# Attention and a gated MLP on one core: every dense product, the scores and P V moved into 64x64 tiles of TensorE, with a new order of the work

## The chip, the cores and the metric

The kernel runs on one core of one Trainium2 chip. The metric is the device time of one launch in microseconds (us). Before the change the median of three runs is 158.33 us (157.89 to 158.91).

## The reference, cut to what matters

S is 2048 tokens of D = 448, in bf16. There are H = 16 heads of 28 columns, each token attends to itself and to seven earlier tokens at distances 2, 4, ..., 14, and F is 1792.

```python
xn = layernorm(x)                               # (x - mean) / sqrt(var + 1e-5)
qkv = xn @ wqkv                                 # q, k, v of 16 heads
logits = q . k[pos - 2 * (0..7)] / sqrt(28)     # -1e9 where that position is negative
o = softmax(logits) @ v ;  s = o @ wo
g = silu(gelu(xn @ w1 + b1) @ w2 + b2)
return x + s * g
```

## The kernel before, in words

**Layout.** Even and odd tokens are kept in two halves of 1024 positions, so that the dilation of 2 becomes a window of eight neighbours. There are 16 token tiles of 128 rows and four chunks of 512 tokens (four tiles each).

**Dense work.** D = 448 is three and a half times 128. Products with that contraction (the projections `qk_rows` L526 and `vproj` L550, and the first layer `ff1` L585) therefore run as seven half steps of 64 rows. `pair` (L477) runs two jobs at once, one in the upper and one in the lower 64 rows of the array, each writing all 128 columns to its own PSUM bank. After four steps the two jobs swap halves, and so banks: since two row tiles must not write one bank at the same time, the second part waits for the first one's last products. The signal goes through a no-op on another engine's queue (`told`, L489 to L493): TensorE tells the no-op's engine, which tells TensorE back. `HOPS` (L20) says whose queue: GpSimd alone for chunks 0 and 1, SyncE or GpSimd later. `first_batch` (L504) starts tiles 0 and 1 in the full array, as their weights land. The second layer (`ff2_part` L616) and the output product (`final_part` L792) have contractions of 14 and 4 times 128 and run in the full array, one product a step.

**Attention.** The tokens are cut into nine blocks of four windows of 57 (one of 56) queries; a window sees 64 keys. For a block, `scores_of` (L666) makes 64 products of 57 columns with 32 rows and 64 columns of the array each (one head's 28 rows padded to 32), into four banks. ScalarE takes their exponential (L687), VectorE or GpSimd multiplies by the mask (L693, `MASK_ON` L21), and `values_of` (L697) makes 64 products for P V in tiles of 64 rows by 32 columns. The value tile holds a column of ones beside each head, so that the sum of the weights comes out with the product; `output_of` (L713) brings that sum to the right partitions with two 32x32 transposes and a reciprocal on VectorE and multiplies (L719 to L733). Values are copied by DMA from token tiles to window tiles (`dma_sb` L352, issued on GpSimd's queue, line L354 in the profile). `VISITS` (L24) groups scores and P V into visits, to change the tile shape seldom.

**What sets the order.** Every step is a task with a cost, dependencies, buffers and a priority, given to `_Plan` (L45). A greedy list scheduler (`run`, L89) picks the order on each engine once, and `emit` (L146) writes the instructions in that order. Each engine then runs its queue in order: an instruction that waits holds all behind it. The priorities stand in `PRIO` and `LATER` (L270 to L294). The chip's own times play no part after that.

**Queues that the change touches.** SyncE issues the loads, the DMA transposes of `xn` and of q and k (`dma_T`, L358) and the stores. GpSimd's queue holds in the beginning: the identity, the bias load (L347), memsets (L319), the mask patterns (L839 to L846), the value copies (L354), the reciprocal roots of tiles 4 to 15 (L425, L426), and the no-ops (L490).

Of the kernel before, what the change touches and what calls it, by code (L numbers as in the profile page):

```python
# [8 lines left out]
F32 = mybir.dt.float32  # L9
BF16 = mybir.dt.bfloat16  # L10
ALU = mybir.AluOpType
# [6 lines left out]
TILED = 30  # L18
SAME = 20
HOPS = ("POOL", ("SP", "POOL"))  # L20
MASK_ON = (("DVE", "POOL"), (0.4, 1.2))  # L21


def VISITS(bs):  # L24
    out = [[("S", b)] for b in bs[:2]]
    for i, b in enumerate(bs):
        out.append([("P", b)] + [("S", c) for c in bs[i + 2:i + 3]])
    return out
# [11 lines left out]
class _Task:  # L40
    __slots__ = ("eng", "cost", "deps", "fn", "prio", "take", "give", "slots",
                 "start", "end", "on", "ndep", "users", "tail", "seq", "table", "limit", "mode", "out")


class _Plan:  # L45
# [7 lines left out]
    def add(self, eng, cost, fn, deps=(), prio=0, take=(), give=(), tail=0.0, table=(), limit=None,  # L53
            mode=128):
# [5 lines left out]
        t.mode, t.out = mode, None  # L60
# [27 lines left out]

    def run(self):  # L89
# [6 lines left out]
        self.mode = 128  # L96
        ready = [t for t in self.tasks if not t.ndep]
        order = []
        while ready:
# [14 lines left out]
            tiled = first[2] == "PE" and self.mode < 64  # L114
            at, t, e, c = min(near, key=lambda k: (-k[1].prio - (TILED if tiled and k[1].mode < 64 else SAME if k[2] == "PE" and k[1].mode == self.mode else 0),
# [4 lines left out]
            if e == "PE" and t.fn is not None:  # L120
                self.mode = t.out or t.mode
# [43 lines left out]
def kernel(  # L165
# [67 lines left out]
    v_tok = [sb(f"v_tok{t}", [P, H, 32]) for t in range(9)]  # L233
    v_tok = v_tok[8:] + v_tok[1:8] + v_tok[:8]
    oT = sb("oT", [P, KT, S])
# [4 lines left out]
    m_gen, m_first, m_mid = [sb(n, [P, 2, 4, NW]) for n in ("m_gen", "m_first", "m_mid")]  # L240
    m1 = [sb(f"m1_{i}", [P, 2, NW]) for i in range(3)]
# [4 lines left out]
    def ring(name, n, shape, dt=BF16, fifo=False):  # L246
# [4 lines left out]
    p_E = ring("E", 8, [P, 512], fifo=True)  # L251
    p_dt = ring("dt", 2, [P, 512], F32)
# [10 lines left out]
    p_v = ring("v", 6, [P, H, 32], fifo=True)  # L263
# [7 lines left out]
        "project": (49.5, 205, 104, 52.5,),  # L271
        "project2": (147, 150, 101, 61,),
        "values": (89.5, 62.5, 21, 58,),
        "attn": (185, 179.5, 78, 174.5, 106.5, 106, 138.5, 136.5, 32.5,),
        "ff1": (185, 180, 84.5, 176.5, 66.5, 64.5, 156.5, 189.5, 203, 146, 76, 114.5, 77.5, 179.5,
            75.5, 118.5, 180.5, 14.5, 163, 68, 151, 115.5, 194.5, 167.5, 180, 188.5, 86, 93,),
        "gelu": (62.5, 22.5, 95, 92.5,),
        "ff2": (144, 162.5, 103.5, 142.5, 44.5, 112.5, 67, 5, 89, 106.5, 101.5, 75, 74, 55, 11.5,
            6.5,),
        "final": (140, 19.5, 70.5, 47, 112, 34.5, 23.5, 142.5, 73, 53, 198.5, 188.5, 81.5, 126.5,  # L280
            180, 71,),
        "norm": (37.5, 132, 179.5, 129.5, 74.5, 99, 161, 69, 63, 62, 43.5, 73, -5.5, 90, 133.5,
            150,),
        "loads": (166.5, 166, 188, 139.5, 54.5,),
        "stats": (47.5, -60, 180.5, 23, 127, 56, 188.5, 77, 197.5, -13.5, 185, 205.5, 138, 14, 52.5,
            138.5,),
        "turn_x": (108.5, -1, 28, 116, 210, 116.5, 131.5, 160, 41.5, 79.5, 70, 119, -4.5, 74.5,
            132.5, 111,),
        "turn_qk": (68.5, 112, 174.5, 90, 80, 6, 149.5, 60.5, 4, 140.5, 199.5, 96.5, 103, 166.5,
            140, 156,),  # L290
        "move_v": (81.5, 95, 23, 95, 18.5, 26.5, 8, 128, 29.5,),
        "copies": (50, 119.5, 58.5, 76, 32.5, 135.5, 43, 1, 87, 79.5, 129, 77, 32, 41.5, 135,),
    }
    LATER = {"swap": 135, "qk": 165, "v": 29.5, "gelu": 30.5, "exp": 55.5, "mask": -60, "pv": 45, "recip": -16.5, "os": 54.5, "y": 153.5, "tanh": 182.5, "g": 58, "sg": 183, "o": 120.5}  # L294
# [45 lines left out]
    t_vw = [plan.add("DVE", 0.08, memset("vector", v[:, :, DH:], 1.0), [t_on], prio=96) for v in v_tok[:9]]  # L340
# [4 lines left out]
    def dma(eng, dst, src, kb, prio, deps=(), issue=0.5, rate=350.0):  # L345
        def fn(_):
            {"SP": nc.sync, "ACT": nc.scalar, "POOL": nc.gpsimd}[eng].dma_start(dst, src)  # L347
        a = plan.add(eng, issue, fn, [t_on] + list(deps), prio)
        return plan.add("DMA", kb / rate, lambda _: None, [a], prio, tail=1.7)
# [16 lines left out]
    def load_x(t0, n, prio, eng="SP", deps=()):  # L366
        d = dma(eng, x_sb[:, t0:t0 + n, :],
                rows(x_half, t0 * P, n * P).rearrange("(t p) d -> p t d", p=P), 112 * n, prio, deps,
                rate=270.0 if t0 < TPC else 350.0)
# [11 lines left out]
    def load_w(kt, prio):  # L381
        t_w.append([dma("SP", w_in[:, kt, :], A_wqkv[kt * P:(kt + 1) * P, :], 336, prio, rate=270.0)])
# [6 lines left out]
    t_w.append([dma("SP", w_in3[:64], tails[:, 0:3:2, :], 112, PRIO["loads"][3], rate=270.0),  # L389
                dma("SP", w_in3[64:], tails[:, 1:3, :], 112, PRIO["loads"][3], rate=270.0)])  # L390

    t_b1z = plan.add("POOL", 0.1, memset("gpsimd", b1r[:], 0.0), [t_on], prio=99)
    t_b1r = dma("POOL", b1r[:NMT], B_b1.rearrange("(m f) -> m f", f=P), 4, 94.5, [t_b1z])
    t_b1r.tail = 5.0
# [41 lines left out]
    def norm(t, prio):  # L436
# [12 lines left out]
        for i in range(2):  # L449
            def f3(k, i=i):  # L450
                xn, tp = buf(p_xn, a), half_bank(buf(p_b, (halves or [k])[0]))
                for kt in (2 * i, 2 * i + 1):
                    nc.tensor.transpose(tp[:, kt, :], xn[:, kt * P:(kt + 1) * P], ident[:])
            halves.append(plan.add("PE", 0.13 if t else 0.22, f3, [twice if i else a, t_ident] + halves, prio, take=() if i else (p_b,),
                                   give=((p_xn, a, 0),) if i else (), tail=0.15))
# [13 lines left out]

    def together(top, bottom):  # L470
        return [(f(), g()) for f, g in zip(top, bottom, strict=True)]
# [5 lines left out]
    def pair(a, b, prio, early=False):  # L477
# [5 lines left out]
        def f1(k):  # L483
# [3 lines left out]
                     tail=0.15, mode=64)  # L487

        def f2(k):  # L489
            held["told"] = (nc.gpsimd if k.on == "POOL" else nc.sync).nop()  # L490
            for i in held["last"]:
                behind(held["told"], i)
# [474 lines left out]
```

## Time and profile before

| what | value |
|---|---|
| median of three runs | 158.33 us (157.89 to 158.91) |
| the profiled execution's own time | 157.98 us |
| its span (first to last instruction) | 156.2 us |
| TensorE busy | 150.1 us, 2204 products |
| VectorE busy | 113.2 us |
| ScalarE busy | 83.3 us |
| GpSimd busy | 74.7 us |
| first layer's first product (L591) | starts at 13.24 us |
| first scores visit (L677) | starts at 45.55 us |
| last TensorE product | ends at 151.7 us |

"Busy" counts time in which the engine works on an instruction. PE is TensorE, PEld its weight loads, DVE VectorE, ACT ScalarE, POOL GpSimd, SP SyncE. A line such as L627 is the line of the kernel that made the instruction; for helpers (L319 memset, L347 and L354 DMA) it is the helper's line. A product's duration in the rows (some 350 ns) is its latency. Products overlap, so the pace is read from start to start.

### The profile page before, as it was taken

Reading aid. Unit: us, or ns where it says so; the run is one execution under the profiler, and the core shown is the slowest. Engines: PE = TensorE matmul, PEld = TensorE weight load, DVE = VectorE, ACT = ScalarE, POOL = GpSimd, SP = SyncE. Lnnn points to the kernel's source line nnn. Section 1 sums busy time; section 2 is a strip of 40 time slices with the busy share of each in tenths; the row PEclk is TensorE's granted clock in tenths of the full one; section 3 lists DMA queues with packets and bytes.
Section 4 is the critical chain, followed back from the end, with each engine's and each line's share of the span. In section 5 each row is a group of like instructions: output and inputs, shape, how many; then the busy total and the mean of one; then the engine's idle time right before and its main releaser. Section 6 shows DMA issues by size and latency. Waiting matters only on the chain.

```text
span 156.2 us, 5305 instructions
## 1 busy us (share of the span) xinstructions
PE 150.1 (96%) x2204; PEld 77.8 (50%) x2204; DVE 113.2 (72%) x259; ACT 83.3 (53%) x149; POOL 74.7 (48%) x123
## 2 busy tenths in 40 slices
PE   6999999999999999999999999999999999999980
PEld 2544454444455555455554644455556444545570
DVE  4789551486266758997799895109899996998992
ACT  3245867378889416444634149782496587051220
POOL 7854856000459408839261098389599780000000
PEclk9999999999999999999999999999999999999999
DMA  4999969999749443099039822123300100200211
GB/s 156 329 317 315 167 124 187 237 269 307 141 95 166 64 82 90 10 192 138 4 83 85 131 70 73 38 76 83 105 0 4 34 31 29 63 4 0 68 36 43
DMA packets 33575, 17.36 MB, mean 111 GB/s; under 512 B 25331, under 2 KB 32387, under 8 KB 33552
## 3 DMA queue, kind: packets, MB, share of 16 engines
q1 hardware_dynamic: 31472, 14.03, 41.3%
q0 software_dynamic: 1936, 2.88, 8.5%
q8 instruction: 17, 0.28, 0.8%
q10 hardware_dynamic: 144, 0.11, 0.2%
q14 instruction: 6, 0.05, 0.1%
HBM read 7.06 MB, written 1.84 MB: 57 GB/s over the span
## 4 chain that ended last, share of the span: by engine, by line
PE 80%; DVE 8%; DMA 3%; POOL 2%; issue 2%; ACT 1%; SPq 1%; DVEq 0%; ACTq 0%; POOLq 0%
PE bank L627 23%; PE bank L591 22%; PE bank L532 11%; PE bank L796 7%; PE bank L556 6%; PE bank L677 4%; PE bank L709 4%; PE bank L327 3%; DMA xnT<-xn 3%; POOL v L354 2%; DVE sg L801 2%; DVE o L807 1%; DVE w_in L659 1%; ACT E L687 1%; DVE xn L438 1%
## 5 line engine op out<-in xcount | busy, mean ns | idle before, releaser
L627 PE MATMUL bank<-w,h 128*128 128x448 bf16 (+1 forms) x238 | 45.2, 342 | 0.0
L591 PE MATMUL bank<-xnT,w 64*128 64x512 bf16 x392 | 44.7, 376 | 0.0
L595 ACT ACTIVATE h<-bank,b 128x512 bf16<-128x512 f32 x56 | 34.0, 689 | 12.9 <-PE bank L591 12.8
L354 POOL DMA_DIRECT2D v<-v_tok x52 | 27.6, 538 | 19.8 <-PE bank L709 9.0
L693 POOL TENSOR_TENSOR E<-E,m_gen 128x456 bf16<-128x456 bf16 x24 | 26.7, 1139 | 11.7 <-ACT E L687 9.5
L627 PEld LDWEIGHTS <-h 128*128 128x128 bf16 x238 | 22.3, 98 | 18.1 <-issue 0.4
L591 PEld LDWEIGHTS <-w 64*128 64x128 bf16 x392 | 19.1, 94 | 22.7 <-issue 1.1
L532 PE MATMUL bank<-w_in,xnT 64*128 64x448 bf16 (+1 forms) x212 | 24.3, 350 | 0.1
L687 ACT ACTIVATE E<-bank 128x456 bf16<-128x456 f32 (+1 forms) x36 | 17.0, 555 | 9.1 <-PE bank L677 9.1
L655 ACT ACTIVATE t<-y 128x448 f32<-128x448 f32 x15 | 8.7, 578 | 17.4 <-DVE y L649 17.4
L719 DVE STREAM_TRANSPOSE dt<-bank 128x480 f32<-128x480 f32 (+1 forms) x18 | 12.1, 671 | 5.6 <-PE bank L709 5.6
L532 PEld LDWEIGHTS <-xnT 64*128 64x128 bf16 (+1 forms) x212 | 10.6, 94 | 10.9 <-issue 1.1
L314 DVE CAST qk_tok<-bank 128x448 bf16<-128x448 f32 x16 | 9.4, 613 | 6.8 <-PE bank L532 6.8
L796 PE MATMUL bank<-wo,oT 128*128 128x448 bf16 (+1 forms) x68 | 14.1, 342 | 0.0
L312 ACT CAST qk_tok<-bank 128x448 bf16<-128x448 f32 x16 | 8.3, 533 | 10.6 <-PE bank L532 10.0
L556 PE MATMUL bank<-w_in,xnT 64*128 64x448 bf16 (+1 forms) x106 | 13.4, 349 | 0.0
L649 DVE TENSOR_TENSOR y<-bank,b 128x448 f32<-128x448 f32 x15 | 9.3, 620 | 4.9 <-PE bank L627 4.9
L728 DVE STREAM_TRANSPOSE dt<-rd 128x480 f32<-128x480 f32 (+1 forms) x18 | 12.1, 673 | 0.5
L733 DVE TENSOR_TENSOR oT<-bank,dt 128x456 bf16<-128x456 f32 (+1 forms) x18 | 11.3, 630 | 0.5
L404 DVE BATCH_NORM_STATS2 st<-x_sb 128x6 f32<-128x448 bf16 x16 | 9.6, 603 | 2.4 <-DMA x_sb<-in_A_x_dram 2.4
L438 DVE TENSOR_SCALAR xn<-x_sb,mv,rstd 128x448 bf16<-128x448 bf16 x16 | 6.3, 394 | 6.0 <-POOL rstd L426 5.8
L796 PEld LDWEIGHTS <-oT 128*128 128x128 bf16 x68 | 6.3, 98 | 6.3 <-issue 0.8
(62 smaller groups left out, 128.9 us busy)
## 6 DMA issues: line engine op xcount, KB each, us to landing
out_dram<-o SPq DMA_DIRECT2D x15, 112.0 KB, 1.7
w<-in_B_w_dram SPq DMA_DIRECT2D x2, 784.0 KB, 7.2
w<-in_B_w_dram SPq DMA_DIRECT2D x2, 672.0 KB, 7.0
x_sb<-in_A_x_dram SPq DMA_DIRECT2D x3, 448.0 KB, 6.3
v<-v_tok POOLq DMA_DIRECT2D x20, 64.0 KB, 2.5
w_in<-in_A_wqkv_dram SPq DMA_DIRECT2D x3, 336.0 KB, 4.3
w<-in_B_w_dram SPq DMA_DIRECT2D x4, 112.0 KB, 6.5
wo<-in_A_wo_dram POOLq DMA_DIRECT2D x4, 98.0 KB, 4.2
```

Of the source, the lines that this page charges most:

```text
L354: nc.gpsimd.dma_start(dst(k), src())
L532: return nc.tensor.matmul(ps[:, :D], xnT[r, kt, cs], w, start=start, stop=stop)
L556: return nc.tensor.matmul(ps[:, :D], xnT[r, kt, k0:k0 + P], w, start=start, stop=stop)
L591: return nc.tensor.matmul(ps[:], w1[r, kt, ms], xnT[r, kt, cs], start=start, stop=stop)
L595: nc.scalar.activation(buf(p_h, own, i)[:], buf(p_b, own, i)[:], ACT.Gelu_apprx_tanh, bias=b1[:, mt:mt + 1])
L627: nc.tensor.matmul(ps[:, :n], buf(*h_at[(c, mt)])[:, j * P:(j + 1) * P], w2[:, mt, cs], start=(mt == 0 and not biased), stop=(mt == NMT - 1))
L687: nc.scalar.activation(buf(p_E, k)[:, :n], buf(p_b, a, at + hl)[:, :n], ACT.Exp, scale=SCALE)
L693: (nc.gpsimd if k.on == "POOL" else nc.vector).tensor_tensor(out=E[:, :n], in0=E[:, :n], in1=m[:, :n], op=ALU.mult)
L719: nc.vector.transpose(buf(p_dt, k)[:, :32 * m], buf(p_b, po, i)[:, :32 * m])
L728: nc.vector.transpose(buf(p_dt, d)[:, :32 * m].rearrange("p (b c) -> p b c", c=32), buf(p_rd, r)[:, :m].unsqueeze(2).to_broadcast((P, m, 32)))
L733: nc.vector.tensor_tensor(out=oT[:, :, q0:q0 + 2 * nq], in0=buf(p_b, po, i)[:, :n].rearrange("p (l q) -> p l q", l=4), in1=buf(p_dt, d)[:, ...
L796: nc.tensor.matmul(ps[:, :n], oT[:, kt, t * P:(t + 1) * P], wo[:, kt, cs], start=(kt == 0), stop=(kt == KT - 1))
```

## The change

- **Dense work.** Each job's product is split into two column strips of 64 (`strips`), and `together` issues the four products of two jobs' strips one after the other: four tiles of 64x64 at a time. The second layer and the output product are made in the same way for two token tiles at once, with the swap of halves and its no-op in between (`rows_in_pairs`, `ff2_pair`, `final_pair`). Tiles 14 and 15 keep the full array there.
- **Scores.** A DMA (`queries_of`, four copies of 32 partitions a block, on SyncE) puts the queries of a block into two planes in which every other head is zero. A scores product then has 64 rows (two heads' keys) and 114 columns (the two planes): 32 products a block instead of 64. The three plane buffers are set to zero at the start on GpSimd.
- **Values.** A value tile has 96 columns for two heads, with 32 zeros between them, so that a P V product of 64 columns adds one head and zeros. The zeros and the ones are set by 18 memsets, 14 of them on GpSimd and four on VectorE, where nine on VectorE were. The window tiles grow from 512 to 768 columns.
- **Masks.** All 36 mask products are on VectorE; 28 were on GpSimd. The mask patterns are 57 columns wide (114 before).
- **Order.** The planner loses the grouping of visits, and gets a term for TensorE's instruction fetch. All priorities are new. Scores and P V are tasks of their own; scores of a block stand two blocks ahead of its P V. The attention output goes into the space of `xnT` and of q in `qkT`, since `oT` is gone. Some of the last output sums go to GpSimd.

The core of the diff:

```diff
-TILED = 30
+BLOCK, FETCH = 128, ((0.0, 4.6), (40.0, 3.8))
-MASK_ON = (("DVE", "POOL"), (0.4, 1.2))
+MASK_ON = ("DVE", 0.4)
...
-    v_tok = [sb(f"v_tok{t}", [P, H, 32]) for t in range(9)]
+    v_tok = [sb(f"v_tok{t}", [P, H // 2, 96]) for t in range(9)]
-    oT = sb("oT", [P, KT, S])
+    p_q = ring("q", 3, [P, 2, G, 4 * NW], fifo=True)
...
-    t_vw = [plan.add("DVE", 0.08, memset("vector", v[:, :, DH:], 1.0), [t_on], prio=96) for v in v_tok[:9]]
+    for n, v in enumerate(v_tok[:9]):
+        e, c = ("DVE", 0.13) if n in (1, 8) else ("POOL", 0.25)
+        for ap, x in ((heads(v[:])[:, :, :, DH:], 1.0), (v[:, :, 32:64], 0.0)):
+            t_vw.append(plan.add(e, c, memset("vector" if e == "DVE" else "gpsimd", ap, x), [t_on], prio=96 if n in (1, 2, 3, 8) else 50))
+    t_q0 = [plan.add("POOL", 1.0, memset("gpsimd", q[:], 0.0), [t_on], prio=20) for q in p_q.bufs]
...
+    def strips(out, lhsT, rhs, half, start, stop):
+        n = P if half > 1 else 64
+        return [lambda c=c: nc.tensor.matmul(out[c:c + n], lhsT[:, c:c + n], rhs, start=start, stop=stop) for c in range(0, P, n)]
     def together(top, bottom):
-        return [(f(), g()) for f, g in zip(top, bottom, strict=True)]
+        done = []
+        for f, g in zip(top, bottom, strict=True):
+            done.append([q() for pair in zip(f(), g(), strict=True) for q in pair])
+        return done
...
+    def queries_of(b):
+        q, nq, _ = VIS[b]
+        def fn(k):
+            to = buf(p_q, k)[:].rearrange("(a b r) z g s -> b a r z g s", a=2, b=2)
+            of = qkT[:, 0, :, q:q + 4 * nq].rearrange("(a b r) g s -> b a r g s", a=2, b=2)
+            for z in range(2):
+                for a in range(2):
+                    nc.sync.dma_start(to[z, a, :, z, :, :4 * nq], of[z, a])
+        a = plan.add("SP", 1.5, fn, [t_qk[t] for t in range(q // P, (q + 4 * nq - 1) // P + 1)] + t_q0, PRIO["move_q"][b], take=(p_q,))
...
     def scores_of(b):
+        def fn(banks, i):
+            for g in range(G):
+                for r in range(2):
+                    for w in range(2):
+                        rs = slice(64 * r, 64 * r + 64)
+                        q0, k0 = wins[w][i]
+                        c0 = 2 * g * nq
+                        nc.tensor.matmul(banks[2 * r + i][NK * w:NK * w + NK, c0:c0 + 2 * nq].rearrange("p (z q) -> p z q", z=2),
+                                         qkT[rs, 1, g, k0:k0 + NK], buf(p_q, at)[rs, :, g, q0 - q:q0 - q + nq], start=True, stop=True)
...
     def values_of(b, exps):
+                        for w in range(2):
+                            rs = slice(NK * w, NK * w + NK)
+                            c0, c1 = (2 * g + i) * nq, (2 * g + z) * nq
+                            nc.tensor.matmul(banks[w][64 * r:64 * r + 64, c0:c0 + nq], v[rs, 2 * g + r, 32 * z:32 * z + 64],
+                                             E[rs, c1:c1 + nq], start=(i, g, z) == (0, 0, 0), stop=(i, g, z) == (1, G - 1, 1))
```

In the changed program's queues TensorE has 3364 products and 6728 instructions with their weight loads (2204 and 4408 before). Of the products 784 are first layer, 618 projections, 826 second layer, 236 output product, 288 scores and 576 P V. SyncE gets 36 more DMAs. On GpSimd the bias load is followed by the memsets of two value tiles, those of `row0` and `wo`, the three mask patterns, the memsets of the other five value tiles and of the three query planes, then the first value copy and the first no-op.

## The prediction, as put on record before the changed kernel ran

> **What bounds the kernel now.** I read the page first (busy shares, slices, chain), then TensorE's timeline, then the queues of the engines that feed it.
>
> ```profile
> span 156.2 us, 5305 instructions
> ...
> PE 150.1 (96%) x2204; PEld 77.8 (50%) x2204; DVE 113.2 (72%) x259; ACT 83.3 (53%) x149; POOL 74.7 (48%) x123
> ...
> PE   6999999999999999999999999999999999999980
> ...
> DVE  4789551486266758997799895109899996998992
> ...
> POOL 7854856000459408839261098389599780000000
> PEclk9999999999999999999999999999999999999999
> ...
> q8 instruction: 17, 0.28, 0.8%
> ...
> PE 80%; DVE 8%; DMA 3%; POOL 2%; issue 2%; ACT 1%; SPq 1%; DVEq 0%; ACTq 0%; POOLq 0%
> ```
>
> TensorE is full from 6 to 151 us and is 80% of the chain that ended last. VectorE is at nine tenths in much of the second half. GpSimd (POOL) is busy in the first 10 us, idle soon after.
>
> TensorE's timeline (start, length) shows what its time is made of:
>
> ```profile
> 49.57 8.12 PE L627 MATMUL bank<-w,h 128*128 128x448 bf16 x42
> 57.62 0.68 PE L709 MATMUL bank<-E,v 64*32 64x57 bf16 x64
> 58.23 0.76 PE L677 MATMUL bank<-qkT 32*64 32x57 bf16 x64
> 58.92 2.82 PE L627 MATMUL bank<-w,h 128*128 128x448 bf16 x14
> ```
>
> From start to start, 42 full-array products take 8.05 us: 0.189 us each and about 0.1 us at the change of tile shape. Row pairs of 512 columns (L591) go at 0.216 us a pair (120 from 29.21 to 42.16). That is 0.42 ns a column, so dense work has no slack. The attention visits are different: 64 products of 57 columns in eight tiles stream for 8 x 0.026 = 0.21 us, yet one takes 0.61 to 0.65. Summed over the timeline (scores to the next dense start), the 18 visits take 12.1 us. 0.4 of it is one wait at 114 us; eleven entries add 0.1 each: 12.7 us of work.
>
> **The change part by part.** The sum is against the profiled execution, 157.98 us, 0.35 under the median of 158.33.
>
> *Dense tiles, 0.* 598 groups of four 64x64 products replace the row pairs and most 128x128 products. A row pair costs what one product costs (0.189 at 448 columns), so I take the same for a four. The ends are 0 and, if the columns of a four did not run beside each other, many us: 1 ns a four is 0.6 us. The eight-tile visits stand against that: their first 32 products run at full streaming rate. A four needs four loads of 64 columns per 189 ns; in a scores visit (L677) 64 such loads go through in 0.63 us, 10 ns apart. The Trainium skill says otherwise on two pages: "TensorEngine Tiling (Array Packing)", Restrictions, says that column tiles lose the fast weight load, and "TensorE: Matmul & The Clock Gate", LDWEIGHTS, gives columns/1.2 ns, 53 for 64. One behind the other, four would take 213 ns, and by that estimate 402 fours of 448 columns lose 9.6 us (166.6 us in all); the row of the visits disagrees.
>
> *Visits, -4.8.* Scores become 32 products of 114 columns in four tiles: 8 rounds of 0.050 = 0.40 us. P V is 64 products in four tiles: 16 x 0.026 = 0.42 us if streaming binds, 0.53 if issue does (0.63 less a shape change). I take 0.48, the middle. 9 x 0.88 = 7.9 for 12.7. Ends 4.3 and 5.3.
>
> *Shape changes between dense runs, -1.05.* The timeline has 15 outside the visits, the new order 4: 11 x 0.095. Ends 0 and -1.05.
>
> *The hop on GpSimd, +3.8.* A pair of jobs swaps banks between its two halves, and a no-op on GpSimd or SyncE (L490) carries the signal; for chunks 0 and 1 it must be GpSimd. What GpSimd does before the first one now:
>
> ```profile
> 1.82 0.70 POOL L347 DMA_DIRECT2D b1r<-in_B_b_dram  x1 [0.30 <-POOL b1r L319]
> 2.52 0.48 POOL L319 MEMSET row<- 128x128 bf16 x2
> 2.95 1.58 POOL L319 MEMSET wo<- 128x1792 bf16 x1
> ...
> 6.14 0.19 POOL L839 MEMSET m<- 128x114 bf16 x1
> ...
> 10.21 0.24 POOL L846 TENSOR_SCALAR_AFFINE_SELECT m<-m 64x56 bf16<-64x56 bf16 x1
> 13.21 1.10 POOL L354 DMA_DIRECT2D v<-v_tok  x2 [2.76 <-PE bank L532]
> ```
>
> ```profile
> L490 POOLq EVENT_SEMAPHORE  x37: 17/17/17, 12.2 to 135.7; - x37
> ```
>
> It is done at 10.45 us and waits for TensorE; the first no-op is at 12.2. In the changed program 14 memsets of value tiles, three of query planes (1824 elements) and one value copy stand ahead of the first no-op. Row by row: 2.5 us to the bias DMA; two value tiles 1.0 (64 elements 0.15 and 256 elements 0.31 by the line through 128: 0.20 and 1792: 1.58, gaps included); rows 0.45; wo 1.55; three masks of 57 columns 1.36 each (6.14 to 7.50), now 4.1; five value tiles 2.5; three planes at 1.6, 4.85; copy 0.53. That is 17.5 to 17.7 us. TensorE has issued the first half of its first w1 pair by 12.9 and of a projection pair by 13.8, and the next instruction in its queue waits for that no-op. So it stands from 13.8 to about 17.6: 3.8 us. Ends: 3.0 (value memsets without gaps) and 5 (short strided runs slower). GpSimd's reciprocal roots for tiles 4 to 7 wait in the same queue behind nine copies and come at 23 and 24 us instead of 18.5 and 19.6. Their transposes then land at 26 to 33 us, about when TensorE, being 3.8 late, asks for them: not added again. If TensorE were not late, this would hold it by about as much. The clock is a risk here: the first nine 512-column products have a mean of 631 ns (L327), 376 later (L591), so it starts slow. The skill's page "TensorE: Matmul & The Clock Gate", Part 1, says that an idle window of some 3.4 us brings half clock back; by that, 3.4 us at half speed add 1.7 us (an estimate), and no run here shows such a gap inside the span.
>
> *Instruction refill, +0.5.* TensorE's program grows from 4408 to 6728 instructions, 17 refills of 16 KB to 26. In the trace refills start as close as 3.65, 3.99 and 4.02 us with no gap in TensorE's work; counted by the 256 instructions between them, the shortest stretch is 4.77. In the new order the densest stretches (a P V visit and dense work) take 3.44, 3.6 and 3.7 us at the rates above. A limit of 3.65 costs 0.3 in sum, 4.0 costs 2.2, 4.75 costs 10.4, and no limit 0. I take 0.5, near the shortest seen.
>
> *Masks on VectorE, +0.6.* GpSimd's 28 mask products go to VectorE: 28 x 0.39 = +10.9 us. Off it come stretched products, as the next two rows show (the same operation beside a GpSimd mask and alone; five such and an output sum, 3.5 us), five output sums (2.0), two casts (1.2), seven memsets (0.8): +3.4 net.
>
> ```profile
> 124.72 1.46 DVE L659 SCALAR_TENSOR_TENSOR w_in<-t,y 128x448 bf16<-128x448 f32 x1
> ...
> 142.41 0.62 DVE L659 SCALAR_TENSOR_TENSOR w_in<-t,y 128x448 bf16<-128x448 f32 x1
> ```
>
> In the attention stage of chunks 0 to 2 (scores 0 to P V 4) VectorE's queue holds some 40 us of work beside 45 of TensorE: nearly full. From scores to P V are 3.4 to 6 us in the new order for six of the nine blocks, 7 or more for all before, and the chain between (four exps 1.9, the last mask 0.39, hand-overs) takes 2.9. So the cover is 0.5 us. I take 0.6 for the stage; ends 0 and 4.
>
> *Query planes and order on SyncE, +0.3.* 36 DMAs of 58 KB, each a 0.33 to 0.5 us issue; a 64 KB copy lands in 2.5 us, and they are issued well ahead. But the second half of w2 now stands behind query copies and transposes that wait for late tiles; I place it at about 56 us, needed at 55. Ends 0 and 3. Value copies grow from 64 to 96 KB, off the path.
>
> *End, -0.3.* The last sums go partly to GpSimd, one 0.28 us step off VectorE's last chain. Ends -0.5 and 0.
>
> Sum: -4.8 - 1.05 + 3.8 + 0.5 + 0.6 + 0.3 - 0.3 = -0.95, so 157.0 us.
>
> **The rivals.** *The hop costs nothing* (chance 0.2): GpSimd's memsets are shorter than the rows say, or later waits of the old start vanish, and 157.0 - 3.8 = 153.2 us. For it: 64- and 256-element strided memsets are not in the trace. Against it: the three planes alone, priced by a row of nearly their length, are 4.8 us of the queue.
>
> *Masks come late* (0.2, the slower side): VectorE at nine tenths puts each block's last mask behind other work, and P V waits. Each of the six tight blocks 0.75 us late is 4.5, less the 0.6 counted: 160.9. It decides from 0.6 us a block on (2.9 us more than the forecast). For it: a cover of 0.5 us. Against it: the stretched products go.
>
> *Refill binds* (0.13): at one block in 4.5 us the stretches lose 7.4, so 163.9; slower from 4.3 us on. Against it: the pairs of refills 3.65 to 4.02 us apart.
>
> *The tiles do not do what is said* (0.05): a four takes 200 ns, 598 x 0.011 = 6.6, so 163.6.
>
> **How the numbers follow.** My forecast, the gain mostly given back at the hop, has 0.42 and its own range 155.2 to 158.9. Cases of both signs hold most of the chance, so the whole range reaches from 152.8 (no hop) to 162.5 (late masks, part of refill), leaving out 0.2. About 1% is what a measurement of this kernel can tell from no change. Faster by more: 0.2 and 0.19 of the forecast's 0.42. Within: 0.21 of it and 0.03 of the slower rivals, where they are mild. Slower: 0.02 of it and the slower rivals' 0.38 less that 0.03. So 0.39, 0.24, 0.37.
>
> **What would show it.** TensorE idle some 4 us near 14 to 18 us, ended by a GpSimd no-op, with GpSimd's memsets until about 17 us: the hop. Visits of 0.40 and 0.42 to 0.53 us and dense fours 0.189 and 0.216 us apart: the gain. Gaps at every 256th instruction with refills evenly spaced: refill. Gaps before P V ended by a VectorE mask: late masks. The forecast is wrong if TensorE runs through 14 to 18 us, or if fours are wider than 0.195 us.

## The result and the profile after

The changed kernel takes 177.51 us in the median of four runs (175.32 to 179.70), the kernel before 158.12. The ratio is 1.1125 [1.1044, 1.1206]: slower by 11%, where 157.0 us was forecast and 162.5 was the upper end. Executions of the changed kernels spread over several per cent, so ratios are of those within 1.5% of a kernel's shortest and medians of all, and the profiled execution of the changed kernel (179.70 us, span 178.0) is its longest.

The page of the changed kernel, the lines that answer to those shown of the kernel before:

```profile
span 178.0 us, 7718 instructions
...
PE 152.5 (86%) x3364; PEld 95.0 (53%) x3364; DVE 121.7 (68%) x275; ACT 83.5 (47%) x151; POOL 54.0 (30%) x113
...
PE   7753999979993974999999799939999999999950
...
PEclk9996599999999997899999999996999999999996
...
q8 instruction: 26, 0.43, 1.2%
...
PE 60%; DVE 11%; DMA 10%; SPq 10%; issue 3%; ACT 2%; POOL 0%; DVEq 0%; ACTq 0%
```

TensorE is no longer full: nine slices between the first and the 28th stand at 3 to 7 tenths, and the clock row falls to 5, 6 and 7 near some of them. In the chain SyncE's queue and transfers now hold 10% each, where they held 1% and 3%.

Part of TensorE's timeline (start, length, products), with the pace of the new tiles:

```profile
40.68 10.75 PE L490 MATMUL bank<-xnT,w 64*64 64x512 bf16 x196
51.26 2.82 PE L490 MATMUL bank<-w_in,xnT 64*64 64x448 bf16 x56
56.75 0.95 PE L490 MATMUL bank<-w_in,xnT 64*64 64x448 bf16 x16 [2.67 <-DMA xnT<-xn]
57.53 0.58 PE L770 MATMUL bank<-q,qkT 64*64 64x114 bf16 x32
57.94 0.74 PE L490 MATMUL bank<-w_in,xnT 64*64 64x448 bf16 x12
```

49 fours of 512 columns go from 40.68 to 51.26: 0.216 us each, as forecast. A scores visit takes 57.94 - 57.53 = 0.41. So the tiles do what was said. What TensorE waited for (us in total, times, longest):

```profile
PE bank L471 <- DVE xn L456: 5.5, 3, 5.0
PE bank L490 <- SPq L515: 4.3, 2, 3.0
PE bank L490 <- DMA xnT<-xn: 3.7, 2, 2.7
PE bank L490 <- SPq L646: 2.2, 1, 2.2
PE bank L803 <- issue: 1.3, 1, 1.3
```

The first is at the start; the next three, 10.2 us, are no-ops and transposed activations that come late from SyncE's queue. That queue around the second of the two waits for `xnT`:

```profile
48.02 3.08 SPq L754 DMA_DIRECT2D q<-qkT  x4
51.14 0.59 SPq L366 DMA_DIRECT2D w<-in_B_w_dram  x1
51.78 3.88 SPq L379 DMA_TRANSPOSE xnT<-xn  x3
55.72 0.58 SPq L366 DMA_DIRECT2D w<-in_B_w_dram  x1
```

Four query copies hold the queue for 3.08 us, a load for 0.59; the transposes start at 51.78, and TensorE stands from 54.08 to 56.75. Beside their own issue, the copies also wait at the head of the queue until the transposes that they read have landed, 7.6 us in five waits, and everything behind them waits too:

```profile
SPq L754 <- DMA qkT<-qk_tok: 7.6, 5, 2.9
```

**The start.** GpSimd's memsets, and VectorE beside them:

```profile
9.55 1.75 POOL L329 MEMSET v_tok<- 128x64 bf16 x10
11.25 4.73 POOL L329 MEMSET q<- 128x1824 bf16 x3
```

```profile
10.07 6.04 DVE L456 TENSOR_SCALAR xn<-x_sb,mv,rstd 128x448 bf16<-128x448 bf16 x1
```

The normalisation of tile 3 takes 6.04 us where its kind takes 0.39. It ends 0.13 us after the last memset, and TensorE stands 4.97 us for it.

**The clock.** The table of stretches, cut at the records of the granted clock (stretch: length, TensorE busy, clock, transfer share, GB/s):

```profile
11.20:14.61 3.41, 0.00 (x1) 1.00 1.06 342
14.61:18.03 3.42, 1.86 (x20) 0.50 0.10 25
18.03:21.44 3.41, 3.41 (x40) 0.50 0.32 59
...
65.81:69.23 3.42, 1.19 (x28) 1.00 1.17 171
69.23:72.64 3.41, 3.41 (x44) 0.50 1.16 169
117.01:120.43 3.42, 1.32 (x28) 1.00 0.63 129
120.43:123.84 3.41, 3.41 (x40) 0.50 0.20 51
```

The changes of clock lie on one grid of 3.41 us. Here a stretch at full clock in which TensorE works 1.32 us or less is followed by one at half clock, whatever is to be done in it. At half clock, 1.86 us of work did not bring the full clock back, 3.41 us did.

**The end.** The closing drain of GpSimd, the longest of the three, before and after (durations in ns, first and last start):

```profile
L962 POOLq DRAIN  x3: 46/92/4805, 135.8 to 155.9; - x3
```

```profile
L1057 POOLq DRAIN  x3: 46/113/5473, 171.7 to 177.7; - x3
```

Before, it runs from 135.8 beside TensorE. After, GpSimd makes two of the last output sums, so its drain starts at 171.7 and ends at 177.2, 2.5 us after SyncE is done.

The difference of the spans, 21.8 us, read from TensorE's rows. "Working" is from the first 64-row product to the last end less the idle time. The last three columns are experiments told below (`split_end`; it without the query copies; the kernel before with such copies).

| us | before | changed | split_end | split_end_none | before_q |
|---|---|---|---|---|---|
| first 64-row product | 10.6 | 16.7 | 11.5 | 10.9 | 11.1 |
| idle after it | 0.3 | 12.0 | 10.1 | 4.7 | 7.2 |
| working | 140.8 | 142.9 | 137.5 | 137.2 | 143.4 |
| from there to the end of the span | 4.5 | 6.4 | 3.8 | 3.6 | 4.7 |

The changed kernel's 142.9 hold half clock; `split_end` had none while it worked, so 5.4 of them are the clock and the tiling itself is worth 137.5 - 140.8 = -3.3. The bill: start +6.1, idle +11.7, clock +5.4, tiling -3.3, end +1.9, together 21.8. It compares one execution of each kernel.

### The profile page after: what moved, and what is told of

Read it like the earlier page. It is cut to its first block, busy times and chain, and to the rows that moved or that the text cites. A ratio compares the mean times of both kernels' runs of the same rounds, so it can differ in the third digit from the quotient of the medians.

```text
span 178.0 us, 7718 instructions
## 1 busy us (share of the span) xinstructions
PE 152.5 (86%) x3364; PEld 95.0 (53%) x3364; DVE 121.7 (68%) x275; ACT 83.5 (47%) x151; POOL 54.0 (30%) x113
## 4 chain that ended last, share of the span: by engine, by line
PE 60%; DVE 11%; DMA 10%; SPq 10%; issue 3%; ACT 2%; POOL 0%; DVEq 0%; ACTq 0%
PE bank L490 51%; SPq L754 6%; DVE xn L456 3%; DMA w_in<-in_A_wqkv_dram 3%; PE bank L700 3%; PE bank L803 3%; SPq L379 3%; DMA xnT<-xn 3%; DMA x_sb<-in_A_x_dram 2%; DVE st L422 2%; PE bank L770 2%; DMA out_dram<-o 2%; SPq L366 1%; ACT E L780 1%; DVE dt L823 1%
## 5 line engine op out<-in xcount | busy, mean ns | idle before, releaser
L490 PE MATMUL bank<-xnT,w 64*64 64x512 bf16 x784 | 47.3, 392 | 3.0 <-SPq L515 3.0
L490 PE MATMUL bank<-w,h 64*64 64x448 bf16 x784 | 42.7, 357 | 2.3 <-SPq L646 2.2
L490 PE MATMUL bank<-w_in,xnT 64*64 64x448 bf16 (+1 forms) x618 | 38.3, 365 | 5.4 <-DMA xnT<-xn 3.7
L490 PEld LDWEIGHTS <-w 64*64 64x64 bf16 x784 | 24.8, 112 | 22.3 <-SPq L515 3.4
L490 PEld LDWEIGHTS <-xnT 64*64 64x64 bf16 (+1 forms) x746 | 23.6, 110 | 21.0 <-DMA xnT<-xn 4.7
L490 PEld LDWEIGHTS <-h 64*64 64x64 bf16 x784 | 24.8, 109 | 14.2 <-SPq L646 2.7
L456 DVE TENSOR_SCALAR xn<-x_sb,mv,rstd 128x448 bf16<-128x448 bf16 x16 | 12.0, 750 | 5.1 <-POOL rstd L444 2.6
L787 DVE TENSOR_TENSOR E<-E,m_gen 128x456 bf16<-128x456 bf16 (+1 forms) x32 | 11.3, 392 | 2.8 <-ACT E L780 2.7
L803 PEld LDWEIGHTS <-v 64*64 64x64 bf16 x576 | 7.4, 108 | 3.2 <-issue 2.0
L803 PE MATMUL bank<-E,v 64*64 64x57 bf16 (+1 forms) x576 | 7.6, 191 | 1.6 <-issue 1.3
```

The costliest lines, as they stand in the source:

```text
L456: nc.vector.tensor_scalar(buf(p_xn, k)[:, :D], x_sb[:, t, :], mv[:, t, 0:1], rstd[:, t:t + 1], op0=ALU.subtract, op1=ALU.mult)
L490: return [lambda c=c: nc.tensor.matmul(out[c:c + n], lhsT[:, c:c + n], rhs, start=start, stop=stop) for c in range(0, P, n)]
L787: (nc.gpsimd if k.on == "POOL" else nc.vector).tensor_tensor(out=E, in0=E, in1=m[:, :, :nq], op=ALU.mult)
L803: nc.tensor.matmul(banks[w][64 * r:64 * r + 64, c0:c0 + nq], v[rs, 2 * g + r, 32 * z:32 * z + 64], E[rs, c1:c1 + nq], start=(i, g, z) == ( ...
```

## The experiments

Theory A: the tiling pays, and three things beside it cost more: memsets that hold VectorE at the start, query copies that make SyncE's queue late, and the half clock that follows. Rival B: refills of instructions bind. Rival F: the new order, not the copies, makes SyncE late. Rival C: tile 3 is late for another reason. Further theories stand in the expectations. Line numbers shift by a few in some of these kernels. The diffs are cut to the lines that matter, and comments in them do not stand in the kernels.

**1. `sets_late`: the memsets after the masks.**

```diff
-            getattr(nc, eng).memset(ap, v)
+            i = getattr(nc, eng).memset(ap, v)
+            if late:                       # planes, five value tiles
+                behind(i, gate_on["m"])    # VectorE's last mask copy
```

> The changed kernel with one edit: the memsets of the three query planes and of five value tiles stay on GpSimd but wait for VectorE's last mask copy, so that none of them lies beside the normalisation of tile 3. Theory A (the memsets held that VectorE operation for 6.04 us, and TensorE's idle time then halved its clock): the operation takes 0.4 us again, the first product of the dense pairs comes at 12 to 13 us instead of 17.8, no clock of 0.5 before 40 us, and the time falls by 5 to 8 us, to 168 to 172. Rival B (the refills of TensorE's instructions bind, so what is won at the start is lost at the next refills): the operation is short but the time falls by less than 2 us. Rival C (tile 3 is late for another reason, its data or its place in VectorE's queue): the operation stays late and the time within 1 us of 177.5.

171.15 us (170.09 to 171.87), ratio 1.082 [1.077, 1.087]: 6.4 less than the changed kernel. The normalisations take at most 0.45 us, the first 512-column four comes at 12.76 (17.83), and no half clock falls into the work. A holds, B and C fall here. And a wait for a GpSimd no-op appears, of the kind that the prediction had counted, but at 20.6 us and behind nine value copies that end at 23.03:

```profile
23.52 0.84 PE L494 MATMUL bank<-xnT,w 64*64 64x512 bf16 x12 [2.93 <-POOLq L519]
```

**2. `sets_split`: two of the planes' memsets behind the second bias's load.**

```diff
+    for t in t_q0[1:]:
+        plan.order.remove(t)
+    n = plan.order.index(t_b2.deps[0]) + 1
+    plan.order[n:n] = t_q0[1:]
```

> The kernel with late memsets, and of its memsets the two query planes that are needed last are moved further back, behind GpSimd's issue of the second bias, where its queue is empty. With the memsets only late, TensorE stood 2.93 us from 20.6 us on for the first hop no-op of GpSimd's queue. If that wait is for the planes (3.2 us of memsets ahead of the no-op), it falls to under 0.6 us and the time by 2 to 3.5 us, from 171.2 to 167.5 to 169. If the nine value copies ahead of the no-op hold it (0.52 us each), the wait stays at over 2 us and the time within 1 us of 171.2.

169.82 us (168.01 to 170.18), 1.071 [1.064, 1.077]. The wait for the no-op falls from 2.93 to 0.95, the time by 1.3, less than expected: what is left of the wait stands behind the value copies, and in the profiled execution TensorE's idle time falls by 2.7 but a stretch at half clock (109.48 to 112.89), which `sets_late` does not have, takes 1.7 back.

**3. `before_sets`: three such memsets in the kernel before.**

```diff
+                if w == first == 1:
+                    for _ in range(3):
+                        nc.gpsimd.memset(oT[:, 0, :1824], 0.0)
```

> The kernel before, with three memsets of 128x1824 that nothing reads (on the tile of the attention output) put between the mask operations of GpSimd, and the copy of the third mask moved behind that of the bias, so that nothing waits for the masks. Theory A: the normalisation of tile 3 beside them takes 3.5 to 5 us instead of 0.39, TensorE idles that much longer near 11 us, the clock is 0.5 for one or two stretches of 3.4 us, and the time is 4 to 8 us longer: 162 to 166. Rival C: 158 to 159.5.

161.22 us (160.50 to 162.13), 1.022 [1.017, 1.027], a little under what theory A expected. VectorE beside 5.01 us of memsets:

```profile
8.99 1.78 DVE L438 TENSOR_SCALAR xn<-x_sb,mv,rstd 128x448 bf16<-128x448 bf16 x1
...
12.40 1.77 DVE L855 COPY m_first<-m 128x456 bf16<-128x456 bf16 x1
```

The memsets alone cost 3.4 us against the runs beside them (157.85) and no clock. VectorE loses about one memset (1.67) at a time, not all of them on one operation as in the changed kernel, and no operation takes the 3.5 us or more that A expected. The Trainium skill's "SBUF — State Buffer", section "SBUF: two separate sides", says that GpSimd and VectorE operations of certain modes share a port pair as an exclusive lock, held for a whole instruction while the other engine is blocked. These rows agree. In the changed kernel one operation lost its turn to some ten memsets in a row (6.04 us, and 5.65 in `q_pool`). It need not: in the profiles of `end_dve`, `dense_wide` and `q_none` the same operation, beside the same memsets, took 0.64, 0.65 and 0.40 us. What decides between the two is open.

**4. `end_dve`: the last output sums on VectorE** (two by the trace: GpSimd makes three where it made five).

```diff
-            eng = nc.gpsimd if k.on == "POOL" else nc.vector
+            eng = nc.gpsimd if k.on == "POOL" and t < NT - 2 else nc.vector
```

> The changed kernel with one edit: the last three additions of the output go to VectorE instead of GpSimd. In the trace of the changed kernel GpSimd's closing drain starts only after its last addition, takes 5.47 us and ends 2.5 us after every other engine is done; in that of the kernel before it takes 4.80 us from 135.79 us on and ends long before. Theory E (the drain is the end): the end comes 2.2 to 2.7 us earlier, 173 to 175.5, and the drain takes 4.8 us beside TensorE's last work. Rival: the drain is as long and as late for whatever was put on GpSimd before, and the time stays within 0.7 us of 177.5.

172.45 us, from 166.71 to 174.77. The profiled execution, 166.71, is one without the stall at the start; the others have no trace, but with mean granted clocks of 0.951 to 0.980 against its 1.000 they probably had it. So the sum can't be read here; the drain can. It starts at 153.1 and takes 4.8 us beside TensorE's work, which ends at 161.16.

**5. `split_end`: 2 and 4 together**, which takes the accident of the start out.

> The kernel with split memsets, and the last three additions on VectorE. It has no race between VectorE and the memsets, so the drain shows alone: 2.2 to 2.7 us less than the 169.8 of the kernel with split memsets, 167 to 168. Rival (the drain is not what ends the run): 169 to 170.5.

166.32 us (164.61 to 167.91), 1.049 [1.045, 1.053], 3.5 less than `sets_split`, more than expected. Theory E holds: the span ends 3.8 us after the last product, not 6.4, and this 2.5 is the drain's part; `sets_split`'s stretch at half clock is missing too. This is the base of what follows.

**6. `q_pool` and `late_pool`: the query copies issued on GpSimd**, in the second with the memsets of 1.

```diff
-                    nc.sync.dma_start(to[z, a, :, z, :, :4 * nq], of[z, a])
+                    nc.gpsimd.dma_start(to[z, a, :, z, :, :4 * nq], of[z, a])
```

> The changed kernel with one edit: the 36 query copies are issued on GpSimd's queue instead of SyncE's, at the same places of the order. Theory A (SyncE spends 0.6 us on the issue of each copy, and the transposes, x loads and hop no-ops queued behind them come late): the gaps of TensorE that end on SyncE's queue or on the transposed activations (1.03, 2.67, 2.23, 1.32 and 2.99 us in the trace of the changed kernel) fall to under 2 us in all, the clock of 0.5 at 69 and 120 us goes, and the time falls by 8 to 13 us, to 164.5 to 169.5. Rival B (refills bind): less than 3 us. Rival D (the copies' waits now hold up GpSimd's own queue, value copies and early no-ops): no better than 175, with gaps that end on GpSimd.

> The changed kernel with both edits: late memsets and the query copies on GpSimd's queue. Theory A: both gains, 13 to 21 us, so 156 to 164, with at most one stretch of half clock left. Rival B (refills bind): 166 to 172, with TensorE's waits now inside visits and dense pairs where no semaphore is late.

176.97 us (174.66 to 180.05), 1.112 [1.104, 1.120], and 175.12 (174.94 to 176.09), 1.111 [1.107, 1.115]. Waits of `q_pool` behind the start:

```profile
PE bank L490 <- issue: 4.3, 2, 3.8
PE bank L490 <- POOLq L646: 4.0, 3, 2.0
```

SyncE's waits are gone and those for `xnT` fall from 3.7 to 1.0, so their place on its queue, not the transfers, had made them late. But GpSimd's no-ops are late instead (D), and for 3.79 us from 71.08 on TensorE waits for a refill: in the trace's records it starts at 71.96, when TensorE already stands, and lands at 73.57. The drain grows by 3 us; in `late_pool`:

```profile
L1066 POOLq DRAIN  x3: 46/98/8413, 165.2 to 174.1; - x3
```

58 transfers issued by GpSimd before, 94 here: 4.80 and, once the 0.61 us of the last sum are taken off, 7.80 us, 0.083 us a transfer in both. So `late_pool` met neither theory: the copies' cost moved to GpSimd's queue, to refills (4.5 us of waits that no semaphore ends) and to the end.

**7. `q_none`, `split_end_none`: no query copies** (the scores multiply zeros), on the changed kernel and on `split_end`.

```diff
-                    nc.sync.dma_start(to[z, a, :, z, :, :4 * nq], of[z, a])
+                    pass
```

> The changed kernel without any of the 36 query copies; the scores multiply the planes' zeros, so the attention is not that of the reference, and every other instruction is there. Theory A (the issue of the copies on SyncE, 0.6 us each, and the transfers behind them cost the waits for no-ops, transposes and x loads): the gaps of TensorE that end on SyncE or on a transfer (10.2 us in the trace of the changed kernel) fall to under 3 us, no stretch of half clock after 40 us, and the time falls by 8 to 13 us, to 164.5 to 169.5. Rival F (the new order itself puts transposes and w2 loads where TensorE needs their queue; the copies only fill it): by less than 4 us.

> Split memsets and additions on VectorE, without the query copies (the scores multiply zeros, so the attention is not the reference's). Theory A: 6 to 8 us less than with the copies, 159.5 to 162, and what is left of TensorE's gaps is of two kinds, GpSimd's no-op near 20 us and waits that no semaphore ends. Rival F (order alone): 164 or more.

The first: 166.62 us (162.94 to 171.98), two groups again, probably by the start. Its profile has no wait for SyncE or a transfer in the work. The second: 160.56 us (156.93 to 165.14, 12 runs), 5.8 less than with the copies by the medians; the ratio, 0.997 [0.994, 1.000], rests on the three shortest of the twelve, and by the ratios it is 8.2 less. Theory A holds, F falls: the same order has no late no-op on SyncE. The longest of TensorE's waits that are left:

```profile
PE bank L494 <- DMA xnT<-xn: 1.7, 2, 1.1
PE bank L807 <- issue: 1.6, 1, 1.6
PE bank L494 <- issue: 0.9, 1, 0.9
```

**8. `before_q`: 36 copies that nothing reads, in the kernel before.**

```diff
+            to = spare[b % 2][:].rearrange("(a b r) g s -> b a r g s", a=2, b=2)
+            of = qkT[:, 0, :, q:q + 160].rearrange("(a b r) g s -> b a r g s", a=2, b=2)
+            for z in range(2):
+                for a in range(2):
+                    nc.sync.dma_start(to[z, a], of[z, a])
```

> The kernel before, with 36 copies on SyncE's queue that nothing reads: for each block four, of 32 partitions and 4 x 160 elements, out of the same tile and issued where that block's transposes have landed by the plan, as in the changed kernel. Theory A (the copies' issues and transfers are the price, in whatever order they stand): SyncE's transposes and no-ops behind them come late, and the time rises by 3 to 8 us, to 161 to 166. Rival F (it is the new order of the work that made them matter; in the order before SyncE has slack): 158 to 159.5.

168.81 us (167.85 to 169.72), 1.068 [1.062, 1.074]: 10.5 us for copies alone, with not one tile changed. SyncE's queue (the first line is that of the kernel before), and what TensorE waits for:

```profile
19.20 5.12 SPq L360 DMA_TRANSPOSE xnT<-xn  x4
...
19.60 3.81 SPq L360 DMA_TRANSPOSE xnT<-xn  x3
23.52 2.70 SPq L945 DMA_DIRECT2D spare<-qkT  x4
26.26 1.29 SPq L360 DMA_TRANSPOSE xnT<-xn  x1
```

```profile
PE bank L532 <- DMA xnT<-xn: 3.1, 2, 1.6
PE bank L591 <- SPq L490: 1.9, 1, 1.9
PE bank L556 <- SPq L490: 1.7, 1, 1.7
```

Before, the four transposes stood in a row from 19.20 to 24.32. Here four copies part the last from the rest, it ends at 27.55, and TensorE stands 1.64 us for it. Near 98 us no-ops come late among eight copies (5.18 us of the queue), and a stretch with 1.50 us of work is followed by half clock. Here no copy waits long for its data, so it is their issue that holds the queue. Rival F is out: in the old order the copies cost at least as much.

**9. `split_end_hops`: every no-op on GpSimd.**

```diff
-            held["told"] = (nc.gpsimd if k.on == "POOL" else nc.sync).nop()
+            held["told"] = nc.gpsimd.nop()
```

> The same, and every hop no-op is issued on GpSimd's queue, where no copy, transpose or load stands ahead of it. Theory A (no-ops come late in SyncE's queue, gaps of 2.63 and 1.37 us in the kernel with split memsets): 3 to 4.5 us less than split memsets with the additions on VectorE, 163 to 165, and no gap ends on SyncE's queue. Rival G (what stands behind the no-ops was waiting for something else as well, transposes or refills): less than 1.5 us.

166.97 us (164.74 to 168.99), 1.047 [1.043, 1.051]: no gain over 166.32. The waits for SyncE (1.9 and 1.6) are gone, but one for a mask grew from 2.0 to 3.3 and waits that no semaphore ends took 2.8; two stretches at half clock in this profile, none in that of `split_end`, add to the difference. The time is as G forecast: something stood close behind.

**10. The planes filled by an engine: `qcopy_pool` (GpSimd) and `qcopy_dve` (VectorE)**, in the first, the later no-ops on SyncE.

```diff
-                    nc.sync.dma_start(to[z, a, :, z, :, :4 * nq], of[z, a])
+                    nc.gpsimd.tensor_copy(to[z, a, :, z, :, :4 * nq], of[z, a])
```

> Split memsets, additions at the end on VectorE, and the query planes filled by GpSimd operations in SBUF in place of transfers; the later hop no-ops all on SyncE. Theory A: without the copies SyncE is as free as in the kernel that left them out, so 158.5 to 162.5, if GpSimd's operations take under 1.5 us each and hold up nothing but the scores. Rival H (GpSimd's operations lie beside VectorE's and one of them waits, as at the start): 164 or more, with VectorE operations of over 1.5 us.

> Split memsets, additions at the end on VectorE, and the query planes filled by VectorE, 36 operations of 32 partitions by 912 elements. By the rows of VectorE's copies (0.18 us for 64 elements, 0.25 to 0.28 for 456) one takes 0.35 to 0.6 us, 13 to 22 us in all on an engine that was busy for 122 of 178. Theory A: 159 to 163. Rival: VectorE becomes the bound in the stretch of the visits, where it also masks and divides, and the time stays at 165 or more.

161.55 us (160.62 to 162.71), 1.022 [1.016, 1.029], and 164.32 (162.21 to 166.62), 1.031 [1.023, 1.039]. On GpSimd:

```profile
L758 POOL COPY q<-qkT 32x912 bf16<-32x912 bf16 (+1 forms) x36 | 35.7, 992 | 4.6 <-PE bank L494 2.2 <-DMA qkT<-qk_tok 0.9
```

35.7 us on an engine that has room, and 4.8 off the time, as theory A expected; the no-ops were moved in the same run, so the two are not told apart. On VectorE, between A and its rival, masks came late (2.9 us of TensorE's waits).

**11. The dense pairs in 64x128 products: `dense_wide`, `split_end_wide`, `split_end_none_wide`**, with half the dense instructions.

```diff
-        n = P if half > 1 else 64
+        n = P
```

> The changed kernel with one part undone: the dense pairs in products of 64 rows by 128 columns as before, two at a time instead of four, so half the instructions for the same work, in the same order. If a four takes what a pair takes (0.216 us at 512 columns, as the trace says) and refills do not bind, the time stays within 1.5 us of 177.5. If the refills of TensorE's instructions cost the changed kernel more than the one gap of 1.29 us at 64 us, it falls by 2 to 5 us with some 7 refills fewer than 26. If four products at a time run faster than two, it rises.

> Split memsets, additions at the end on VectorE, query copies on SyncE as in the changed kernel, and the dense pairs in products of 64 rows by 128 columns. If refills cost where the copies fill the transfer engines, the time falls by over 1.5 us against 166.3; if SyncE's queue decides where TensorE waits, it stays within 1.5 us.

> The same without the copies, and the dense pairs in products of 64 rows by 128 columns, so that half their instructions are gone. Theory B for what is left (refills: the waits that no semaphore ends were 4.6 us in the run without copies): those waits fall to under 1 us and the time by 2 to 4.5 us against the kernel without copies. If a wide pair is slower than a four, or the refills were hidden: within 1 us of it.

171.32 us (170.59 to 173.80; its profile has no stall at the start, so it says little beside 177.5); 165.04 (162.86 to 166.31), 1.036 [1.027, 1.045], 1.3 less than `split_end` by the medians, 2.0 by the ratios; 159.29 (156.98 to 163.09, 11 runs), 1.000 [0.997, 1.003], about level with `split_end_none`. In the profile of the last, the waits that no semaphore ends are gone (2.6 us in that of `split_end_none`). But "working" grows from 137.2 to 139.5 us, because each visit now stands between two changes of tile shape:

```profile
48.65 0.60 PE L778 MATMUL bank<-q,qkT 64*64 64x114 bf16 x32
49.18 0.74 PE L494 MATMUL bank<-w_in,xnT 64*128 64x448 bf16 x6
```

A scores visit takes 0.53 us where it took 0.41, and the dense run ahead of a visit 0.09 more (28 pairs 2.74 us, 28 fours 2.65); over nine scores visits and eighteen entries that is 2.7. So this edit does not show refills alone: it trades them for shape changes of about the same size. The waits that no semaphore ends, read as waits for refills, are 1.3 us in the trace of the changed kernel, 2.6 in `split_end_none` and 4.6 in `q_none`. As the cause of the 19 us B is out; as a cost of the many short products it is not.

**12. `qcopy_pool2` and `qcopy_pool2_wide`: the no-ops of the first layer's pairs on SyncE too.**

```diff
-            held["told"] = (nc.gpsimd if early else nc.sync).nop()
+            held["told"] = (nc.gpsimd if on_pool else nc.sync).nop()   # chunk 0's projections
```

> The kernel that fills the planes with GpSimd operations, and the hop no-ops of the second tile group and of the first layer's pairs are moved from GpSimd's queue, where one came 1.8 us late behind those operations, to SyncE's. If that wait was the no-op's place, 1 to 2 us less than 161.6: 159.5 to 160.6, about the kernel before or still above it (158.3). If the transposes of SyncE's queue (1.2 to 1.3 us each) now hold the no-ops as long: within 0.7 us of 161.6.

> The same, with the dense pairs in products of 64 rows by 128 columns. With few transfers left beside them the refills should be hidden, as they were in the kernel without copies: within 1 us of the run beside it. If it is 1.5 us or more faster, the short products still pay for their instructions. A time under 157.5 would be a kernel that beats both; the sum of TensorE's own time allows 154 to 155 with no wait at all.

165.29 us (163.87 to 165.56), 1.042 [1.038, 1.046], 3.7 more than `qcopy_pool`:

```profile
PE bank L494 <- SPq L519: 7.1, 9, 1.8
```

Nine waits for no-ops behind SyncE's transposes. The wide one: 167.78 (165.23 to 168.81), 1.050 [1.044, 1.055]; in its profile the waits are shorter by 1.4, but the working time is longer by 4.1: 1.7 is a stretch at half clock, and the rest is again the size of the shape changes. No version that computes everything beat the kernel before. The best of them is `qcopy_pool`.

## Why the prediction was wrong, step by step

| step | forecast, us | the trace, us |
|---|---|---|
| dense tiles, visits, shape changes | -5.85 | -3.3 |
| hop at the start | +3.8 | +6.1, by another wait |
| clock | a risk of 1.7, not in the sum | +5.4 |
| refill | +0.5 | +1.3 |
| masks | +0.6 | +0.3 |
| query copies and order on SyncE | +0.3 (0 to 3) | +10.2 |
| end | -0.3 | +1.9 |

**The step that failed is "Query planes and order on SyncE, +0.3".** It counted an issue at 0.33 to 0.5 us, from stores and loads. A copy of 32 partitions takes 0.60 (median of 36), so a block's four hold the queue for 2.4 to 3.1 us, with 7.6 us of waits for their data on top, and the step asked only whether the copies themselves are early enough. It did not ask who is queued behind them: transposes that TensorE needs within a microsecond or two, and the no-ops on which a pair hangs. `before_q` measured it alone: 10.5 us, against an end of 3. Not all of the 10.2 goes with the copies: 1.7 us of waits for `xnT` stay in `split_end_none`, and between `split_end` and that kernel the time differs by 5.8 to 8.2. One of its guesses held: the second half of w2 is issued at 55.72, forecast at about 56.

**The hop** named the right engine, place and instructions, but its mechanism failed too. The memsets ended at 15.98, about 1 us before the 17.0 to 17.2 of its sum, and hurt VectorE beside them first. Where that does not happen they do not hold the no-op either. In `end_dve`, with the same memsets in the same place, the first no-ops are on record at 13.29 and 14.05 us while the memsets run to 16.23, the second half of the first w1 pair starts at 13.73 without a wait, and TensorE runs through 14 to 18 us, which the prediction gave as a sign of being wrong:

```profile
11.37 4.86 POOL L329 MEMSET q<- 128x1824 bf16 x3
16.19 4.71 POOL L373 DMA_DIRECT2D v<-v_tok  x9
...
13.73 0.91 PE L490 MATMUL bank<-xnT,w 64*64 64x512 bf16 x12
21.40 0.84 PE L490 MATMUL bank<-xnT,w 64*64 64x512 bf16 x12 [1.43 <-POOLq L515]
```

What the memsets do hold is the value copies, and a later no-op stands behind nine of these: 1.43 us near 20 us here, 1.71 in `dense_wide`, 2.03 in `q_none`, 2.93 in `sets_late`, where 3.8 was taken. The copies in front of the roots were in the prediction; that they stand in front of a no-op was not.

**The clock** was named as a risk and left out of the sum, since no run showed it. The Trainium skill's page "TensorE: Matmul & The Clock Gate", section "What's actually happening", gives a free-running window of 3413 ns, after one idle of which the clock halves. The grid agrees (3.41 us); the condition does not: 1.19 and 1.32 us of work did not keep the clock up.

**Dense tiles at 0 held**: 0.216 a four, and 0.189 at 448 columns (56 products from 59.83 to 62.48), so the row of the visits was the better guide to the weight loads than the two pages weighed against it. **The visits** were mis-sized: scores take 0.41 as forecast, but P V mostly 0.56 to 0.7 where 0.48 was taken, some 1.1 us in nine: four products start 32 to 33 ns after the four before, not 26. The other 1.4 us of the missing gain were not taken apart. **Masks** held: VectorE's busy time rose by 8.5 us, 5.6 of it the one stretched normalisation, so 2.9 for the +3.4 net. **Refill** stayed within its ends in this execution (1.3 for 0.5), not in all kernels of the same products. **The end** failed: no step looked at what GpSimd does after its last sum, its drain, which the rows of the kernel before show ending long before it matters.

Of the rivals none was near: the slower ones, late masks and refill, are 0.3 and 1.3 us of the bill. The rows are of one execution and rounded, so they add up only nearly to 21.8.

## What to carry to other kernels

Price an added transfer by what stands behind its issue: list the queue's next instructions and when their consumers start, add what the transfer itself must wait for, and measure it by putting the transfer alone into the old kernel. Keep long GpSimd memsets away from the stretch where VectorE makes what TensorE waits for. Count what every queue must still finish after its last useful instruction.

## What the runs showed of the hardware that was not expected

- A VectorE normalisation of 0.39 us took 6.04 beside the last ten or so of thirteen GpSimd memsets in one execution, and 0.64 and 0.40 in others of nearly the same program.
- GpSimd's no-ops can pass while its memsets still run: in `end_dve` at 13.29 and 14.05 us, with memsets to 16.23. Behind value copies they wait: the fifth came at 21.33, after nine copies that ended at 20.90.
- The granted clock is decided for each stretch of 3.41 us by the one before. In the 20 traces, every stretch at full clock with 1.38 us of TensorE's work or less was followed by half clock, every one with 1.51 or more by full clock. Of seven between 1.40 and 1.50, three went to half (1.50 in `before_q`) and four stayed full (1.41 in `sets_late`), so what is counted may be something other than busy time:

```profile
19.19:22.60 3.41, 1.41 (x28) 1.00 0.51 131
22.60:26.01 3.41, 2.48 (x52) 1.00 0.17 49
```

  A gap of 2.67 us cut by the grid (54.08 to 56.75, the boundary at 55.57) cost no clock; one of 2.23 that lay in one stretch did.
- GpSimd's closing drain took 0.083 us for each transfer that it had issued: 4.80 us for 58, 7.80 for 94.
